# MLP first product in pairs of 64-row matmuls, with relays on ScalarE and the transposes moved to the second product

## The chip, the core and the metric

The kernel runs on one core of a Trainium2 chip. The core has a matrix engine (TensorE, PE in the profile; PEld is its weight load), VectorE (DVE), ScalarE (ACT), GpSimd (POOL) and a queue for transfers (SyncE, SP). TensorE writes into PSUM, eight banks of 128 partitions by 512 fp32 numbers; everything else lives in SBUF, 128 partitions wide. The metric is the device time of one execution in microseconds, lower is better. The time before is 827.49 us, the median of three runs (826.62 to 827.83).

## What is computed

Four layers over x of 2048 tokens by D = 576, in the order A, B, A, B. A is linear attention with 32 heads, B is an MLP with F = 4608 hidden units. Both take a layer norm first, and the norm inside B is applied to a row that has been normed already.

```python
def _B_ref(x, w1, b1, w2, b2):
    y = _layernorm(x, axis=-1)
    h = _gelu(jnp.einsum("bsd,df->bsf", y, w1) + b1)
    return jnp.einsum("bsf,fd->bsd", h, w2) + b2

x = x + _A_ref(_layernorm(x, axis=-1), A_wqkv, A_wo)
x = x + _B_ref(_layernorm(x, axis=-1), B_w1, B_b1, B_w2, B_b2)
x = x + _A_ref(_layernorm(x, axis=-1), A_wqkv, A_wo)
x = x + _B_ref(_layernorm(x, axis=-1), B_w1, B_b1, B_w2, B_b2)
```

`_A_ref` makes q, k, v from one product with `wqkv`, takes `phi` (an exponential linear unit plus one) of q and k, forms k-transposed-times-v and the sum of k per head, multiplies q with both, divides, and multiplies with `wo`.

## The kernel before

All products are in bf16 with fp32 sums in PSUM. Tokens are cut into 16 tiles of 128 rows, and for the MLP into four chunks of 512 tokens (`NCB`, `CB`), each of four tiles (`TPC`). D = 576 is held as five blocks of 128 rows (`KD`), of which the last has only 64 real rows. The normed activations stand transposed in one array, `yT`.

**The MLP (`LayerB`).** For each chunk, `m1_group` (line 458) is called for nine groups `g` of four blocks of 128 hidden units (`GF` = 4, `NF` = 36). A block needs four matmuls over 128 rows (line 469, 512 tokens wide) and one over the last 64 rows (line 474, "the tail"). The tail's activations stand in both halves of the partitions, and the tail weights of even blocks stand in rows 0 to 63 and of odd blocks in rows 64 to 127 of `w1_tail`, so that two tails can run side by side in two halves of the array. So a group is sixteen matmuls of 128 rows and then four of 64 rows. Two of the four sums of a group lie in single banks of the pool `ps_h` (three buffers), the other two in a pair of banks, tag `accA` for even and `accB` for odd groups. Four activations on ScalarE (line 478, gelu) take them to `hT`. `hT` shares its one buffer (tag `big`) with the work array `abig` of the attention layer.

Then comes the second product (line 499): for each of the four token tiles `j` of the chunk 36 x 2 matmuls of 288 columns, into the pair `accA` or `accB` by `j % 2`. VectorE adds the residual (line 278), and SyncE stores the row tile.

**The layer norm pipe (`LNPipe`).** A token tile goes through stages, one a `tick()`: load (-1), statistics on VectorE (0), power on GpSimd (1), a product on VectorE (2), the norm on VectorE and a copy of 64 columns on GpSimd (3), and in stage 4 five TensorE transposes into the one buffer `tp` (line 234) and a VectorE copy into `yT` (line 238). Ticks are called after each group of the first product and three times per token tile in the second. The next chunk's tiles are fed at g = 2, 4, 6, 8; their loads use the tag `xn`, which the residual uses as well.

**Order.** The framework's scheduler sorts the instructions of each engine by program order and by its own estimate of when they can start, and sets the semaphores; each engine then runs its list in order. Only the start-up transfers have an order by hand (`chained`). The first two groups of chunk 0 (g = 0 and 1) are issued from within the last steps of the attention layer (`make_a2_hook`), so their matmuls are mixed with the attention's output product (line 426).

Of the kernel before, what the change touches and what calls it, by code (L numbers as in the profile page):

```python
# [7 lines left out]
ACT = mybir.ActivationFunctionType  # L8
ALU = mybir.AluOpType
BF16 = mybir.dt.bfloat16  # L10
F32 = mybir.dt.float32
PSUM = bass.MemoryType.PSUM
DRAM = bass.MemoryType.DRAM

S, D, F, H, DH = 2048, 576, 4608, 32, 18
P = 128
NT = S // P
KD = 5
DPAD = KD * P
NF = F // P  # L20
# [6 lines left out]
NCB = S // CB  # L27
TPC = CB // P
CA = 512
NCA = S // CA  # L30
HALF = D // 2
# [4 lines left out]
def build(tc, A_x, A_wqkv, A_wo, B_w1, B_b1, B_w2, B_b2, out, dbg=None, n_layers=4):  # L36
    nc = tc.nc
    dbg = dbg or {}
    with ExitStack() as ctx:
# [54 lines left out]
        x0_tiles = {}  # L94

        NOSYNC = mybir.DependencyInfo(mybir.DependencyClass.NoSync, mybir.DependencyReason.SCHED_ONLY)
        chain = dict(last=None)

        def chained(inst):
            if chain["last"] is not None:  # L100
                tc.add_manual_dep(inst.ins, chain["last"], NOSYNC, reason="start-up DMA issue order")
            chain["last"] = inst.ins.name
            return inst

        def load_x0(t):
# [69 lines left out]
        class LNPipe:  # L175
# [7 lines left out]
            def busy(self):  # L183
                return len(self.items)

            def tick(self):
                for it in list(self.items):
                    st = it["stage"]
                    if st == -1:
                        xn = work.tile([P, D], F32, name="xn", tag="xn", bufs=3)  # L190
                        nc.sync.dma_start(out=xn[:], in_=x_d[it["load"]])
                        it["xt"] = xn
                    elif st == 0:
                        xt = it["xt"]
                        stt = work.tile([P, 2, 6], F32, name="ln_st", bufs=4)
                        nc.vector.bn_stats(out=stt[:, 0, :], in_=xt[:, 0:HALF])
                        nc.vector.bn_stats(out=stt[:, 1, :], in_=xt[:, HALF:D])
                        mv = work.tile([P, 2], F32, name="ln_mv", bufs=6)
                        nc.vector.bn_aggr(out=mv[:], in_=stt[:])
                        u = work.tile([P, 1], F32, name="ln_u", bufs=4)  # L200
                        if it["kind"] == "A":
                            nc.vector.tensor_scalar(out=u[:], in0=mv[:, 1:2], scalar1=EPS, scalar2=None, op0=ALU.add)  # L202
                        else:
                            nc.vector.tensor_scalar(out=u[:], in0=mv[:, 1:2], scalar1=1.0 + EPS, scalar2=EPS * EPS,
                                                    op0=ALU.mult, op1=ALU.add)
                        it["mv"], it["u"] = mv, u
                    elif st == 1:
                        rstd = work.tile([P, 1], F32, name="ln_rstd", bufs=6)
                        nc.gpsimd.tensor_tensor(out=rstd[:], in0=it["u"][:], in1=neg_half[:], op=ALU.pow)  # L209
                        it["rstd"] = rstd  # L210
                    elif st == 2:
                        nmr = work.tile([P, 1], F32, name="ln_nmr", bufs=4)
                        nc.vector.tensor_scalar(out=nmr[:], in0=it["mv"][:, 0:1], scalar1=-1.0,
                                                scalar2=it["rstd"][:, 0:1], op0=ALU.mult, op1=ALU.mult)
                        it["nmr"] = nmr
                    elif st == 3:
                        y = y_ring[state["ycnt"] % NY]
                        state["ycnt"] += 1
                        xt = it["xt"]
                        if it["norm"] == "act":  # L220
                            nc.scalar.activation(out=y[:, 0:D], in_=xt[:, 0:D], func=ACT.Identity,
                                                 scale=it["rstd"][:, 0:1], bias=it["nmr"][:, 0:1])
                        else:
                            eng = nc.vector if it["norm"] == "dve" else nc.gpsimd
                            eng.tensor_scalar(out=y[:, 0:D], in0=xt[:, 0:D], scalar1=it["rstd"][:, 0:1],
                                              scalar2=it["nmr"][:, 0:1], op0=ALU.mult, op1=ALU.add)
                        nc.gpsimd.tensor_copy(out=y[:, D:DPAD], in_=y[:, 4 * P:D])  # L227
                        it["y"] = y
                    elif st == 4:
                        y = it["y"]  # L230
                        t = it["t"]
                        tp = ps_tp.tile([P, KD, P], BF16, name="tp", tag="tp")
                        for k in range(KD):
                            nc.tensor.transpose(out=tp[:, k, :], in_=y[:, k * P:(k + 1) * P], identity=ident[:])  # L234
                        if it["evac"] == "act":
                            nc.scalar.copy(out=yT[:, :, t * P:(t + 1) * P], in_=tp[:])
                        else:
                            nc.vector.tensor_copy(out=yT[:, :, t * P:(t + 1) * P], in_=tp[:])  # L238
                        self.items.remove(it)
                        continue  # L240
                    it["stage"] = st + 1
# [44 lines left out]
        def layer_A(li, next_kind, pre_a1=None, a2_hook=None):  # L286
# [146 lines left out]
            for s in range(-2, NT + 1):  # L433
# [11 lines left out]
                if a2_hook is not None:  # L445
                    a2_hook(s)

        GF = 4
        NGRP = NF // GF

        class LayerB:
# [5 lines left out]

            def m1_group(self, c, g):
                if c not in self.hT:
                    self.hT[c] = big.tile([P, NF, CB], BF16, name="hT", tag="big")  # L460
                hT = self.hT[c]
                ctok = slice(c * CB, (c + 1) * CB)
                pair = ps_acc.tile([P, 2, 512], F32, name="hp_ps", tag=("accA", "accB")[g % 2])
                hps = [ps_h.tile([P, 512], F32, name="h_ps", tag="h") for _ in range(2)]
                dst = [hps[0][:], hps[1][:], pair[:, 0, :], pair[:, 1, :]]
                for n in range(GF):
                    f = g * GF + n
                    for k in range(KD - 1):
                        nc.tensor.matmul(dst[n], lhsT=w1_sb[:, k, f * P:(f + 1) * P], rhs=yT[:, k, ctok],  # L469
                                         start=(k == 0), stop=False)  # L470
                for n in range(GF):
                    half = slice(64 * (n % 2), 64 * (n % 2) + 64)
                    fc = (g * GF + n) // 2 * P
                    nc.tensor.matmul(dst[n], lhsT=w1_tail[half, fc:fc + P], rhs=yT[half, KD - 1, ctok],  # L474
                                     start=False, stop=True)
                for n in range(GF):
                    f = g * GF + n
                    nc.scalar.activation(out=hT[:, f, :], in_=dst[n], func=ACT.Gelu_apprx_tanh,  # L478
                                         bias=b1T[:, f:f + 1], scale=1.0)
                self.done[c] = g + 1  # L480

            def run(self):
                li, next_kind = self.li, self.next_kind
                for c in range(NCB):
                    for g in range(self.done.get(c, 0), NGRP):
                        self.m1_group(c, g)
                        if g in (3, 5):
                            prefetch_xo(li, c * TPC + (g - 3) // 2, add_b2=True)
                        if c + 1 < NCB and g in (2, 4, 6, 8):
                            t = (c + 1) * TPC + (g - 2) // 2  # L490
                            lnp.feed(None, t, "B", "dve", "dve", load_from=t)
                        lnp.tick()
                    hT = self.hT.pop(c)
                    for j in range(TPC):
                        t = c * TPC + j
                        acc = ps_acc.tile([P, 2, 512], F32, name="m2_ps", tag=("accA", "accB")[j % 2])
                        for f in range(NF):
                            for half in range(2):
                                nc.tensor.matmul(acc[:, half, 0:HALF], lhsT=hT[:, f, j * P:(j + 1) * P],  # L499
                                                 rhs=w2_sb[:, f, half * HALF:(half + 1) * HALF],  # L500
                                                 start=(f == 0), stop=(f == NF - 1))
                            if f % 12 == 6:
                                lnp.tick()
                            if f == 18 and j < 2:
                                prefetch_xo(li, c * TPC + 2 + j, add_b2=True)
# [47 lines left out]
        for li, kind in enumerate(kinds):  # L553
            nk = kinds[li + 1] if li + 1 < n_layers else None
            if kind == "A":
# [9 lines left out]
                while late_pads:  # L565
                    late_pads.pop(0)()
            else:
                lbs[li].run()
        lnp.drain()


# [45 lines left out]
```

## Time and profile before

| | |
|---|---|
| median of three runs | 827.49 us |
| span of the profiled execution | 822.3 us |
| median less span (what lies around the span) | 5.2 us |
| TensorE busy | 799.8 us (97%) |
| ScalarE busy | 326.1 us (40%) |
| VectorE busy | 276.2 us (34%) |
| GpSimd busy | 106.8 us (13%) |
| mean granted TensorE clock | 0.995 |

The page gives no device time of the profiled execution of its own other than its span, so the median is set beside it. A matmul of the profile lasts longer than the distance to the next one, because matmuls overlap in the array: 379 ns is the length of a 512-column matmul, and the starts of two in a row are 216 ns apart. A busy share of 97% therefore hides whatever gap is shorter than that overlap; the starts have to be read.

### The profile page before, as it was taken

Reading aid. Unit: us, or ns where it says so; the run is one execution under the profiler, and the core shown is the slowest. Engines: PE = TensorE matmul, PEld = TensorE weight load, DVE = VectorE, ACT = ScalarE, POOL = GpSimd, SP = SyncE. Lnnn points to the kernel's source line nnn. Section 1 sums busy time; section 2 is a strip of 40 time slices with the busy share of each in tenths; the row PEclk is TensorE's granted clock in tenths of the full one; section 3 lists DMA queues with packets and bytes.
Section 4 is the critical chain, followed back from the end, with each engine's and each line's share of the span. In section 5 each row is a group of like instructions: output and inputs, shape, how many; then the busy total and the mean of one; then the engine's idle time right before and its main releaser. Section 6 shows DMA issues by size and latency. Waiting matters only on the chain.

```text
span 822.3 us, 14103 instructions
## 1 busy us (share of the span) xinstructions
PE 799.8 (97%) x5844; PEld 510.9 (62%) x5878; DVE 276.2 (34%) x850; ACT 326.1 (40%) x600; POOL 106.8 (13%) x198
## 2 busy tenths in 40 slices
PE   5999999999999999999999999999999999999998
PEld 3787774486458547744877877536844863585376
DVE  5756974024204502310244598543201200010000
ACT  5687745501530351046027767452045015303510
POOL 6420301012102301210100000121200010011000
PEclk9999999999999999999999999999999999999999
DMA  9990543013002300100110035722200110011000
GB/s 229 280 299 1 174 132 107 0 59 102 15 1 68 106 1 29 59 29 1 59 58 1 2 95 181 225 64 60 64 22 15 42 47 0 1 55 34 0 23 22
DMA packets 42896, 56.81 MB, mean 69 GB/s; under 512 B 10256, under 2 KB 26896, under 8 KB 42832
## 3 DMA queue, kind: packets, MB, share of 16 engines
q1 hardware_dynamic: 42832, 55.91, 22.8%
q8 instruction: 46, 0.75, 0.4%
q14 instruction: 18, 0.15, 0.1%
HBM read 39.38 MB, written 16.52 MB: 68 GB/s over the span
## 4 chain that ended last, share of the span: by engine, by line
PE 88%; DVE 3%; ACT 3%; issue 1%; DMA 1%; POOL 1%; ACTq 0%; DVEq 0%; POOLq 0%
PE m_ps L499 33%; PE h_ps L469 15%; PE hp_ps L469 15%; PE q_ps L335 5%; PE k_ps L303 4%; PE wo_ps L426 3%; PE h_ps L474 3%; PE v_ps L314 2%; PE v_ps L311 2%; PE hp_ps L474 2%; ACT hT L478 2%; PE tp L234 2%; PE to_ps L416 1%; PE kvacc L327 1%; PE nd_ps L389 1%
## 5 line engine op out<-in xcount | busy, mean ns | idle before, releaser
L499 PE MATMUL m_ps<-w_sb,hT 128*128 128x288 bf16 x2304 | 287.9, 286 | 2.5 <-ACT hT L478 2.5
L499 PEld LDWEIGHTS <-hT 128*128 128x128 bf16 x2304 | 224.1, 98 | 59.9 <-issue 4.5
L478 ACT ACTIVATE hT<-h_ps,b1T 128x512 bf16<-128x512 f32 x144 | 91.2, 684 | 340.2 <-PE h_ps L474 340.2
L469 PEld LDWEIGHTS <-w_sb 128*128 128x128 bf16 x1152 | 107.9, 98 | 139.1 <-issue 21.7
L469 PE MATMUL hp_ps<-yT,w_sb 128*128 128x512 bf16 x563 | 135.5, 379 | 0.7
L469 PE MATMUL h_ps<-yT,w_sb 128*128 128x512 bf16 x555 | 134.8, 380 | 1.1
L478 ACT ACTIVATE hT<-hp_ps,b1T 128x512 bf16<-128x512 f32 x144 | 91.3, 694 | 0.0
L209 POOL TENSOR_TENSOR ln_rstd<-ln_u,neg_half 128x1 f32<-128x1 f32 x64 | 36.6, 572 | 371.3 <-DVE ln_u L202 219.8
L238 DVE COPY yT<-tp 128x640 bf16<-128x640 bf16 x40 | 19.6, 490 | 186.5 <-PE tp L234 186.5
L268 POOL TENSOR_TENSOR xo<-xo,b_bc 128x576 f32<-128x576 f32 x32 | 41.1, 1283 | 206.5 <-DMA xo<-x_d 206.4
L278 DVE TENSOR_TENSOR xbf<-m_ps,xo 128x576 bf16<-128x576 f32 x16 | 12.1, 754 | 141.7 <-PE m_ps L499 141.7
L335 PE MATMUL q_ps<-yT,wqkv_sb 128*126 128x512 bf16 (+1 forms) x200 | 51.7, 381 | 0.0
L426 PE MATMUL wo_ps<-wo_sb,abig 128*128 128x288 bf16 x320 | 46.7, 286 | 0.0
L303 PE MATMUL k_ps<-wqkv_sb,yT 128*128 128x288 bf16 x320 | 46.3, 293 | 0.0
L278 DVE TENSOR_TENSOR xn<-m_ps,xo 128x576 f32<-128x576 f32 x16 | 12.1, 758 | 99.2 <-PE m_ps L499 99.2
L251 ACT ACTIVATE phi_e<-k_ps 128x288 bf16<-128x288 f32 x64 | 26.8, 419 | 38.9 <-PE k_ps L303 35.6
L256 DVE TENSOR_TENSOR abig<-phi_a,phi_e 128x288 bf16<-128x288 bf16 (+2 forms) x104 | 36.0, 346 | 8.1 <-ACT phi_a L253 2.2
L254 DVE TENSOR_SCALAR phi_e<-phi_e 128x288 bf16<-128x288 bf16 (+2 forms) x104 | 29.7, 286 | 21.7 <-ACT phi_e L251 21.3
L426 PEld LDWEIGHTS <-abig 128*128 128x128 bf16 x320 | 29.6, 98 | 10.7 <-issue 1.3
L303 PEld LDWEIGHTS <-yT 128*128 128x128 bf16 x320 | 30.7, 100 | 8.0
L234 PE MATMUL tp<-ident,y_ring 128*128 128x128 bf16 x320 | 29.2, 222 | 4.5 <-POOL y_ring L227 1.9
L234 PEld LDWEIGHTS <-y_ring 128*128 128x128 bf16 x320 | 21.6, 99 | 18.1 <-issue 11.5
(73 smaller groups left out, 651.9 us busy)
## 6 DMA issues: line engine op xcount, KB each, us to landing
x_d<-xn SPq DMA_DIRECT2D x48, 288.0 KB, 2.2
xo<-x_d SPq DMA_DIRECT2D x48, 288.0 KB, 2.9
xn<-x_d SPq DMA_DIRECT2D x24, 288.0 KB, 3.0
w_sb<-in_B_w_dram SPq DMA_DIRECT2D x6, 864.0 KB, 11.0
xbf<-in_A_x_dram SPq DMA_DIRECT2D x32, 144.0 KB, 4.1
w_sb<-in_B_w_dram SPq DMA_DIRECT2D x9, 512.0 KB, 5.2
out_dram<-xbf SPq DMA_DIRECT2D x16, 144.0 KB, 1.8
wqkv_sb<-in_A_wqkv_dram SPq DMA_DIRECT2D x1, 1152.0 KB, 6.7
```

Source lines behind the costliest of these rows:

```text
L209: nc.gpsimd.tensor_tensor(out=rstd[:], in0=it["u"][:], in1=neg_half[:], op=ALU.pow)
L234: nc.tensor.transpose(out=tp[:, k, :], in_=y[:, k * P:(k + 1) * P], identity=ident[:])
L254: nc.vector.tensor_scalar(out=e[0:rows, 0:n], in0=e[0:rows, 0:n], scalar1=1.0, scalar2=1e-6, op0=ALU.min, op1=ALU.add)
L256: nc.vector.tensor_tensor(out=out_ap, in0=a[0:rows, 0:n], in1=e[0:rows, 0:n], op=ALU.max)
L268: nc.gpsimd.tensor_tensor(out=xo[:], in0=xo[:], in1=b2_bc[:], op=ALU.add)
L303: nc.tensor.matmul(kp[:, 0:HALF], lhsT=yT[:, k, tok], rhs=wqkv_sb[:, k, D + half * HALF: D + (half + 1) * HALF], start=(k == 0), stop=(k = ...
L335: nc.tensor.matmul(qp[0:GR[g], :], lhsT=wqkv_sb[:, k, GO[g]:GO[g] + GR[g]], rhs=yT[:, k, c * CA:(c + 1) * CA], start=(k == 0), stop=(k == ...
L426: nc.tensor.matmul(wp[:, half, 0:HALF], lhsT=oT[:, k, :], rhs=wo_sb[:, k, half * HALF:(half + 1) * HALF], start=(k == 0), stop=(k == KD - 1))
L469: nc.tensor.matmul(dst[n], lhsT=w1_sb[:, k, f * P:(f + 1) * P], rhs=yT[:, k, ctok], start=(k == 0), stop=False)
L474: nc.tensor.matmul(dst[n], lhsT=w1_tail[half, fc:fc + P], rhs=yT[half, KD - 1, ctok], start=False, stop=True)
L478: nc.scalar.activation(out=hT[:, f, :], in_=dst[n], func=ACT.Gelu_apprx_tanh, bias=b1T[:, f:f + 1], scale=1.0)
L499: nc.tensor.matmul(acc[:, half, 0:HALF], lhsT=hT[:, f, j * P:(j + 1) * P], rhs=w2_sb[:, f, half * HALF:(half + 1) * HALF], start=(f == 0), ...
```

## The change

The first product is issued entirely as matmuls of 64 rows. Each 128-row block becomes an upper half (rows 0 to 63) and a lower half (rows 64 to 127), and the tail goes to the half in which its weights stand: nine half matmuls per block, 36 per group, eighteen for each half of the array. They are issued alternately, upper and lower. The upper half takes the blocks in the order 0, 1, 2, 3 and the lower in the order 2, 3, 0, 1, so that at any moment they write different banks. Midway in the group the halves exchange banks. The hand-over is guarded by two one-column copies on ScalarE per group ("relays"): a relay waits for the matmul that ends the first use, and the first matmuls of the second use wait for the relay.

TensorE's instructions of the MLP are put into program order by hand (`pe`). The pairs `accA` and `accB` now alternate throughout (`next_acc`), so the second product's first tile does not take the pair that the last group used. Transposes are not issued in the ticks of the first product any more, and at most one token tile is transposed in a tick of the second. The next chunk's tiles are fed at g = 4 and 6 and in the second product at j = 0, f = 6 and 18, and their loads have a tag of their own (`xl`, two buffers).

```diff
+        relay_sb = const.tile([P, 2], F32, name="relay_sb")
+        nc.gpsimd.memset(relay_sb[:], 0.0)
...
+        def pe(inst):
+            if pe_chain["on"]:
+                if pe_chain["last"] is not None:
+                    tc.add_manual_dep(inst.ins, pe_chain["last"], NOSYNC, reason="TensorE order in the MLP")
+                pe_chain["last"] = inst.ins.name
             return inst
...
-            def tick(self):
+            def tick(self, transposes=1):
                 for it in list(self.items):
                     st = it["stage"]
+                    if st == 4:
+                        if transposes == 0:
+                            continue
+                        transposes -= 1
                     if st == -1:
-                        xn = work.tile([P, D], F32, name="xn", tag="xn", bufs=3)
+                        xn = work.tile([P, D], F32, name="xl", tag="xl", bufs=2)
...
+        def next_acc():
+            acc_turn["n"] += 1
+            return ("accA", "accB")[acc_turn["n"] % 2]
...
-                for n in range(GF):
+                def half_blocks(n, hi):
                     f = g * GF + n
-                    for k in range(KD - 1):
-                        nc.tensor.matmul(dst[n], lhsT=w1_sb[:, k, f * P:(f + 1) * P], rhs=yT[:, k, ctok],
-                                         start=(k == 0), stop=False)
...
+                    rows = slice(64 * hi, 64 * hi + 64)
+                    ops = [(n, w1_sb[rows, k, f * P:(f + 1) * P], yT[rows, k, ctok]) for k in range(KD - 1)]
+                    if f % 2 == hi:
+                        fc = f // 2 * P
+                        ops.append((n, w1_tail[rows, fc:fc + P], yT[rows, KD - 1, ctok]))
+                    return ops
+
+                upper = [op for n in (0, 1, 2, 3) for op in half_blocks(n, 0)]
+                lower = [op for n in (2, 3, 0, 1) for op in half_blocks(n, 1)]
...
+                relay_at = {last[(0, 0)]: (0, 2), last[(1, 3)]: (1, 3)}
+                starts = {first[(1, 0)]: 0, first[(0, 2)]: 2, first[(1, 1)]: 1, first[(0, 3)]: 3}
+                for i, (hi, n, wt, mv) in enumerate(order):
+                    mm = pe(nc.tensor.matmul(dst[n], lhsT=wt, rhs=mv, start=(seen[n] == 0), stop=(seen[n] == 8)))
+                    seen[n] += 1
+                    if i in starts:
+                        tc.add_manual_dep(mm.ins, relay_of[starts[i]], SYNC, reason="row tiles take turns on a PSUM bank")
+                    if i in relay_at:
+                        relay = nc.scalar.copy(out=relay_sb[:, 1:2], in_=relay_sb[:, 0:1])
+                        tc.add_manual_dep(relay.ins, mm.ins.name, SYNC, reason="row tiles take turns on a PSUM bank")
+                        for m in relay_at[i]:
+                            relay_of[m] = relay.ins.name
+                    if seen[n] == 9:
+                        f = g * GF + n
+                        nc.scalar.activation(out=hT[:, f, :], in_=dst[n], func=ACT.Gelu_apprx_tanh,
+                                             bias=b1T[:, f:f + 1], scale=1.0)
...
-                        if c + 1 < NCB and g in (2, 4, 6, 8):
-                            t = (c + 1) * TPC + (g - 2) // 2
-                            lnp.feed(None, t, "B", "dve", "dve", load_from=t)
-                        lnp.tick()
+                        if g in (4, 6):
+                            feed_next(c, (g - 4) // 2)
+                        lnp.tick(transposes=0)
...
-                        acc = ps_acc.tile([P, 2, 512], F32, name="m2_ps", tag=("accA", "accB")[j % 2])
+                        acc = ps_acc.tile([P, 2, 512], F32, name="m2_ps", tag=next_acc())
...
                             if f % 12 == 6:
+                                if j == 0 and f in (6, 18):
+                                    feed_next(c, 2 + f // 18)
                                 lnp.tick()
```

## The prediction

> **What bounds the kernel now.** I read the page's busy shares first, then the chain that ended last, then single stretches of the order of time, because only starts show what TensorE loses.
>
> ```profile
> PE 799.8 (97%) x5844; PEld 510.9 (62%) x5878; DVE 276.2 (34%) x850; ACT 326.1 (40%) x600; POOL 106.8 (13%) x198
> ...
> PE 88%; DVE 3%; ACT 3%; issue 1%; DMA 1%; POOL 1%; ACTq 0%; DVEq 0%; POOLq 0%
> ...
> L499 PE MATMUL m_ps<-w_sb,hT 128*128 128x288 bf16 x2304 | 287.9, 286 | 2.5 <-ACT hT L478 2.5
> L474 PEld LDWEIGHTS <-w_tail x288: 92/93/96, 118.4 to 782.2; 64*128 64x128 bf16 x144
> ```
>
> TensorE is the bound everywhere that the change touches; the other engines are below half. A gain must come out of TensorE's own list. One group of the first product in order of time, chunk 1 of the first MLP:
>
> ```profile
> 203.00 3.13 PEld L469 LDWEIGHTS <-w_sb 128*128 128x128 bf16 x16 [0.42 <-issue]
> 203.01 1.90 PE L469 MATMUL h_ps<-yT,w_sb 128*128 128x512 bf16 x8
> ...
> 204.74 1.89 PE L469 MATMUL hp_ps<-yT,w_sb 128*128 128x512 bf16 x8
> ...
> 206.56 0.11 PEld L474 LDWEIGHTS <-w_tail 64*128 64x128 bf16 x4 [0.42 <-issue]
> 206.57 0.39 PE L474 MATMUL h_ps<-yT,w_tail 64*128 64x512 bf16 x2
> 206.79 0.38 PE L474 MATMUL hp_ps<-yT,w_tail 64*128 64x512 bf16 x2
> 206.99 1.27 ACT L478 ACTIVATE hT<-h_ps,b1T 128x512 bf16<-128x512 f32 x2 [1.61 <-PE h_ps L474]
> 207.10 0.28 PEld L234 LDWEIGHTS <-y_ring 128*128 128x128 bf16 x5 [0.42 <-issue]
> 207.10 0.45 PE L234 MATMUL tp<-ident,y_ring 128*128 128x128 bf16 x5
> ```
>
> The reader is to see three things. Eight matmuls in 1.89 us, of which the last lasts 0.38, are 7 steps of 0.216. Two tails lie side by side: both pairs last as long as one matmul, and the pairs are 0.22 apart. And each change between 128 and 64 rows leaves a gap that the busy row hides: the eighth matmul starts at 204.74 + 1.89 - 0.38 = 206.25 and the first tail at 206.57, 0.31 later where 0.216 would do; from the second pair (206.79) to the transposes (207.10) again 0.31. So a change of rows costs some 0.094 us. Last, the seam from first to second product:
>
> ```profile
> 161.84 0.78 PE L499 MATMUL m_ps<-w_sb,hT 128*128 128x288 bf16 x5
> 162.33 0.10 PEld L234 LDWEIGHTS <-y_ring 128*128 128x128 bf16 x1
> 162.58 0.44 PE L234 MATMUL tp<-ident,y_ring 128*128 128x128 bf16 x5
> 162.59 1.27 ACT L478 ACTIVATE hT<-hp_ps,b1T 128x512 bf16<-128x512 f32 x2
> 162.86 0.65 PE L499 MATMUL m_ps<-w_sb,hT 128*128 128x288 bf16 x4
> 163.91 1.26 PE L499 MATMUL m_ps<-w_sb,hT 128*128 128x288 bf16 x9 [0.40 <-ACT hT L478]
> ```
>
> TensorE starts again 0.05 us after ScalarE's last gelu (162.59 + 1.27 = 163.86): group 8 and tile 0 share a pair of banks.
>
> **The change part by part.** The sum is made against the span of the one profiled execution, 822.3 us; the median of the runs, 827.49, is 5.2 above, and I carry that over as it is.
>
> *Matmul work.* Before, a group is 16 + 2 steps of 0.216 = 3.89 us; after, 18 pairs, also 3.89 if a pair takes one step. Nothing is saved here. Does a pair take one step? The two tail pairs start 227 ns apart, but the first step after any change of rows is longer in full-row rows too (226 for 216; transposes 66 for 56), so about 1 ns is left over. That is one step per group, and no row shows a long train of pairs. I take 2 ns a pair, 72 groups x 18 x 2 ns = +2.6 us; the ends are 0, and 10 ns (all of that longer step), +13.
>
> *Weight loads.* 36 a group for 20, one per 0.108 us. Transposes show loads 0.056 apart (five in 0.28), and all four tail loads are issued and done in 0.11 us, two of them for halves whose matmul had just begun. So they hide behind the matmuls: nothing. The Trainium skill, "TensorE: Matmul & The Clock Gate", Part 3, says otherwise: a weight load overlaps a matmul in flight only if it goes to another row group. By that rule each pair would expose a load of 93 ns, 1296 x 0.093 = +120 us, and the kernel would end near 940. The rows above contradict it, for full rows as well (each L469 load lies beside a matmul of the same rows), and I go by the rows.
>
> *Changes of rows removed.* The starts show 74 changes to 64 rows and 73 back, 147 x 0.094 = 13.8 us. After, each of eight chunks has one in and one out (16). The groups 0 and 1 in the attention's tail stay mixed with 128-row work; before, their matmuls come in about nine pieces between attention work, now every piece in 64 rows costs two changes: some 10 per layer, 20. Saved (147 - 36) x 0.094 = -10.4 us; ends -8 and -12.3.
>
> *The seam.* `next_acc` gives tile 0 the pair of group 7, whose gelus are long over. Gaps of the kind shown, over eight chunks: 3.5 us before line 499 and 1.9 us before the transposes of line 234 that wait there for `tp` or for their row. -5.4 us; ends -3.5 and -5.4. What is late next at the seam is the gelu of the last four blocks, needed by tile 0's f = 32, 64 matmuls x 0.1225 = 7.8 us later.
>
> *The relays.* 144 one-column copies on ScalarE. No row shows one; exponentials of 288 and 512 columns take 419 and 600 ns, a straight line through them gives 0.19 us at no columns. ScalarE has time (2.3 + 0.4 of 3.9 us a group), so the question is lateness, since both halves of the array stand behind a waiting matmul and ScalarE works in order. Clock a group from its first pair. ScalarE starts 0.41 us after the start of the matmul it waits for (206.57 to 206.99). Block 0 ends with the lower step 12: gelu at 2.59 + 0.41 = 3.01; the four gelus run 0.57 to 0.59 apart, so the last starts at 4.74, and relay 1 of the next group at 5.32, that is 1.43 on its clock (its own matmul, step 4, would let it go at 1.28). It ends by 1.62 to 1.74 (a gelu's end trails by 0.12), TensorE may go 0.05 later, at the latest at 1.79. It is wanted at step 9, 1.94. Relay 2 waits for step 8: 1.73 + 0.41 + 0.19 + 0.05 = 2.38, wanted at step 13, 2.81. So nothing, with 0.15 us and 0.43 us to spare; the first is the thinnest cover of the change. Beyond it every 0.1 us costs 64 groups (those behind another group) x 0.1 = 6.4 us. Upper end: 0.1 late, +6.4.
>
> *The groups within the attention's tail.* Relays stand in ScalarE's list with copies of 0.69 us (line 418), and gelus of group 0 can't start before `abig` is free (129.89 in the first layer). Group 1's second matmul now needs the pair `accB`, free only after the last residual (128.56 + 0.77 = 129.3); before, four matmuls of its block 0 could go ahead. And its relay 1 stands behind group 0's gelus, 129.89 + 4 x 0.575 + 0.24 = 132.4, where step 9 would come at 129.4 + 1.94 = 131.3. So up to 1 us and 1.1 us are lost per layer, +4 us for the two; lower end 0 (the earlier attention work moves up by as much), upper end +8.
>
> *Transposes, loads, order.* The same 40 groups of five transposes at 0.28 us; in the second product they change no rows. Ticks there are 24 x 0.1225 = 2.94 us apart. The tightest is the next chunk's fourth tile, whose norm stands behind another tile's transposes (0.28), a copy (0.49, after 0.25), its norm (0.57) and GpSimd's copy (0.24) with some 0.2 of hand-over: 2.0 of 2.94 us. The 24 loads (3.0 us to landing) move later on SyncE's queue; the fourth waits for the first-used `xl` buffers, and VectorE may stand up to 2 us for it in tile 0, ahead of tile 0's residual, whose pair is wanted only a tile (9 us) later. Nothing on the path; if the cover fails it is 0.67 us a seam, as before at 636.6, 4 us over six. The memset at the start is hidden by the wait for the first transfers.
>
> Sum: +2.6 - 10.4 - 5.4 + 0 + 4 + 0 = -9.2 us: span 813.1, time 818.3.
>
> **The rivals.**
> *Late relays (slower).* If ScalarE's chain from step 12 to step 9 of the next group is longer than I reckon, each group waits. It decides from 9.2 / 64 = 0.14 us of lateness, that is 0.3 us more than reckoned. Against it: every term but the copy is a row; for it: the margin is only 0.15. At 0.3 us late the time is 818.3 + 19 = 837; had a gelu of the same group come ahead of relay 2, it would be near 1 us a group, 880.
> *Pairs do not keep the step.* Break-even is (9.2 + 2.6) / 1296 = 9 ns a pair. At 20 ns: 818.3 + 23 = 842. For it: there are only two pairs in a row anywhere. Against: the second pair's 1 ns.
> *The hand-over brings the gap back.* If TensorE, held at a waiting matmul, can't load the lower half's weights in advance, a load (0.093) shows at one or both relays: +6 to +12, 824 to 830, about no change. Against: a satisfied wait costs nothing at line 469 now, and after the wait at 163.91 the next matmul follows at the usual distance.
> *It does not do what it says* (a copy between gelus makes ScalarE reload its tables, 1.28 us twice per relay): near 1100. The profile has four reloads, none at a copy.
>
> **How the numbers follow.** The forecast 0.62, with its own range 811 to 824 (sum of the low ends -12.3 - 5.4 = -17.7, and a few us up); the hand-over 0.11; late relays 0.11; pairs 0.12; the rest 0.04. About 0.2% (1.7 us) can be told from no change. Faster: 0.62, most of the hand-over, and small lateness, 0.73; same 0.05; slower 0.22. The range goes from 810 to 833, which leaves out the worse parts of relays and pairs.
>
> **What would show it.** Right: in a group no gap between rows, 18 pairs at 0.216 (3.89 us from group to group for 4.09 now), starts of upper and lower a few ns apart, no wait of the matmul for a relay, the second product following the last pair at about 0.31, transposes only among line 499. Wrong: TensorE waiting for ScalarE at step 9, pairs at 0.23 or more, or several us more than now between the attention's last product and group 2.

## The result: 908.4 us, slower by 9.8%, and one wait that was not in the sum

The changed kernel takes 908.41 us (median of 907.11 to 910.56) against 827.44 us, a ratio of 1.0984 with an interval of 1.0965 to 1.1003. The prediction was 818.3 us with a range to 833. The profiled execution has a span of 906.6 us for 822.3 before.

The page of the changed kernel, the lines that answer to those shown of before (busy time and share of each engine; the chain that ended last; groups of instructions with busy time, mean ns and the idle time ahead of them):

```profile
PE 801.6 (88%) x7030; PEld 538.2 (59%) x7030; DVE 270.4 (30%) x850; ACT 356.9 (39%) x746; POOL 106.2 (12%) x199
...
PE 79%; ACT 11%; DVE 4%; issue 2%; DMA 1%; POOL 1%; DVEq 0%; POOLq 0%; ACTq 0%
...
L513 PE MATMUL hp_ps<-yT,w_sb 64*128 64x512 bf16 x1152 | 274.1, 376 | 81.4 <-ACT hT L524 81.4
L551 PE MATMUL m_ps<-w_sb,hT 128*128 128x288 bf16 x2304 | 289.8, 286 | 0.0
```

TensorE is as busy as before (801.6 us for 799.8), so the work has not grown. What is new is idle time: 81.4 us ahead of the half matmuls into the pair of banks (`hp_ps`), ended by ScalarE's gelu (line 524). The chain of waits shows the same: ScalarE's share went from 3% to 11%. The seam, on the other hand, is clean: line 551, the second product, has no idle time ahead of it, where line 499 had 2.5 us.

The list of waits tells how often (us in total, times, longest):

```profile
PE hp_ps L513 <- ACT hT L524: 81.4, 72, 1.4
ACT relay_sb L518 <- PE hp_ps L513: 48.3, 72, 0.9
```

72 times is once a group. One group in order of time, the end of group 0 of chunk 1 in the first MLP (TensorE's and ScalarE's lines):

```profile
216.76 0.19 ACT L518 COPY relay_sb<-relay_sb 128x1 f32<-128x1 f32 x1 [0.68 <-PE hp_ps L513]
...
217.36 0.38 PE L513 MATMUL hp_ps<-yT,w_tail 64*128 64x512 bf16 x1
217.36 0.38 PE L513 MATMUL h_ps<-yT,w_sb 64*128 64x512 bf16 x1
217.56 0.69 ACT L524 ACTIVATE hT<-h_ps,b1T 128x512 bf16<-128x512 f32 x1 [0.62 <-PE h_ps L513]
218.15 0.68 ACT L524 ACTIVATE hT<-hp_ps,b1T 128x512 bf16<-128x512 f32 x1
218.88 0.37 PE L513 MATMUL hp_ps<-yT,w_sb 64*128 64x512 bf16 x1 [1.14 <-ACT hT L524]
218.89 0.39 PE L513 MATMUL h_ps<-yT,w_sb 64*128 64x512 bf16 x1
```

The pair at 217.36 is step 13 (the steps of a group are its 18 pairs, counted from 0): the upper half ends block 2 with its tail, the lower half begins block 1. Then TensorE stands until 218.88, the next step coming 1.52 us after this one where 0.216 would do: 1.30 us lost. It starts 0.05 us after the end of the gelu that reads block 2 (218.15 + 0.68 = 218.83). The relays have nothing to do with it: the second one was over at 216.95. So the matmul that waits is step 14, the first with which the upper half goes on with block 3, and it waits for the gelu of block 2. The two blocks lie in different banks, but in one PSUM tile, `pair`. 72 x 1.30 = 93.6 us, and 908.4 - 93.6 = 814.8.

The stages tell the same without the single wait. Read off the order of time, from the first matmul of one part to the first of the next, in us:

| kernel | first product, chunk 1 of MLP 1 | all of chunk 1, MLP 1 | all of chunk 1, MLP 2 | group 0 to the end of chunk 0, MLP 1 |
|---|---|---|---|---|
| before | 37.78 | 75.08 | 73.96 | 84.19 |
| after | 46.90 | 84.52 | 83.40 | 97.21 |

46.90 less nine times 1.30 is 35.2, and nine groups of 18 steps of 0.216 are 35.0.

### The profile page after: what moved, and what is told of

Its sections match the earlier page's. It is cut to its first block, busy times and chain, and to the rows that moved or that the text cites. A ratio compares the mean times of both kernels' runs of the same rounds, so it can differ in the third digit from the quotient of the medians.

```text
span 906.6 us, 16729 instructions
## 1 busy us (share of the span) xinstructions
PE 801.6 (88%) x7030; PEld 538.2 (59%) x7030; DVE 270.4 (30%) x850; ACT 356.9 (39%) x746; POOL 106.2 (12%) x199
## 4 chain that ended last, share of the span: by engine, by line
PE 79%; ACT 11%; DVE 4%; issue 2%; DMA 1%; POOL 1%; DVEq 0%; POOLq 0%; ACTq 0%
PE m_ps L551 31%; PE h_ps L513 15%; PE hp_ps L513 15%; ACT hT L524 10%; PE q_ps L351 4%; PE k_ps L319 3%; PE v_ps L330 2%; PE wo_ps L442 2%; PE v_ps L327 2%; PE tp L250 2%; DVE xn L294 1%; PE kvacc L343 1%; PE to_ps L432 1%; DVE o_ring L416 1%; PE nd_ps L405 1%
## 5 line engine op out<-in xcount | busy, mean ns | idle before, releaser
L513 PE MATMUL hp_ps<-yT,w_sb 64*128 64x512 bf16 x1152 | 274.1, 376 | 81.4 <-ACT hT L524 81.4
L513 PE MATMUL h_ps<-yT,w_sb 64*128 64x512 bf16 x1152 | 286.0, 377 | 0.0
L513 PEld LDWEIGHTS <-w_sb 64*128 64x128 bf16 x2304 | 137.5, 94 | 215.0 <-issue 104.5
L518 ACT COPY relay_sb<-relay_sb 128x1 f32<-128x1 f32 x144 | 27.4, 190 | 272.5 <-PE h_ps L513 224.0
L524 ACT ACTIVATE hT<-hp_ps,b1T 128x512 bf16<-128x512 f32 x144 | 98.4, 683 | 78.7 <-PE h_ps L513 78.7
L524 ACT ACTIVATE hT<-h_ps,b1T 128x512 bf16<-128x512 f32 x144 | 98.4, 683 | 45.0 <-PE h_ps L513 43.3
L513 PE MATMUL h_ps<-yT,w_tail 64*128 64x512 bf16 x144 | 54.1, 376 | 0.0
L513 PE MATMUL hp_ps<-yT,w_tail 64*128 64x512 bf16 x144 | 54.1, 376 | 0.0
L243 POOL COPY y_ring<-y_ring 128x64 bf16<-128x64 bf16 x64 | 15.4, 244 | 228.5 <-DVE y_ring L241 199.1
```

The costliest lines, as they stand in the source:

```text
L513: mm = pe(nc.tensor.matmul(dst[n], lhsT=wt, rhs=mv, start=(seen[n] == 0), stop=(seen[n] == 8)))
L518: relay = nc.scalar.copy(out=relay_sb[:, 1:2], in_=relay_sb[:, 0:1])
```

## The experiments

**The two theories.** A: the framework orders the accesses to a PSUM tile by the tile, not by the bank; a matmul that follows, in program order, a gelu on the other bank of its tile waits for that gelu. In the changed kernel the gelu of block 2 is issued as soon as block 2 has its nine halves (step 13), ahead of block 3's last four matmuls. B: the wait belongs to the hand-over of banks through the relays, wherever the blocks lie. The built program speaks for A; it names what each instruction waits for (abridged, in its order, steps 13 and 14; `hp_ps[0:]` and `hp_ps[512:]` are the two banks of one tile):

```
Matmult     hp_ps[0:]   upper, step 13, last of block 2
Matmult     h_ps        lower, step 13, first of block 1    its load waits for relay 2
Activation  hT<-hp_ps[0:]   gelu of block 2
Matmult     hp_ps[512:] upper, step 14, block 3             waits for: Activation hT<-hp_ps[0:]
```

**Blocks regrouped (e1_regroup).** The pair holds blocks 1 and 3, which both end in step 17.

```diff
-                dst = [hps[0][:], hps[1][:], pair[:, 0, :], pair[:, 1, :]]
+                dst = [hps[0][:], pair[:, 0, :], hps[1][:], pair[:, 1, :]]
```

> The changed kernel, but the pair of banks holds blocks 1 and 3 of a group (which both end with step 17) and the two single banks hold blocks 0 and 2. Theory A (block 3's last four matmuls wait for the gelu of block 2 because both lie in one PSUM tile and the framework orders accesses tile by tile): the 72 waits of 1.30 us go, 908.4 - 93.4 = 815 us, 812 to 820; groups 3.89 us apart. Theory B (what is late is the relay of the second hand-over, wherever the blocks lie): the wait before block 3 stays, 908 us. If relay 1 is late by what I reckoned as its thin margin, some us more than 815 and a wait at step 9.

Measured: 908.38 us (907.85 to 908.9), no gain at all in the time. By that number alone it is theory B. The trace says something else: the wait is no longer at step 14. It stands now before the very last half matmul of a group, the tail of block 1.

```profile
PE hp_ps L513 <- ACT hT L524: 77.9, 72, 3.3
...
222.66 0.69 ACT L524 ACTIVATE hT<-hp_ps,b1T 128x512 bf16<-128x512 f32 x1
223.40 0.37 PE L513 MATMUL hp_ps<-yT,w_tail 64*128 64x512 bf16 x1 [0.86 <-ACT hT L524]
```

In step 17 the upper half's matmul ends block 3, its gelu is issued at once, and only then comes the lower half's matmul, which ends block 1, in the same tile. Program order between two matmuls of one step was enough. That the time came out the same to 0.03 us is chance: the wait is a little shorter (the first product of chunk 1 takes 46.10 us for 46.90), and the granted TensorE clock was a little lower (0.990 to 0.992 in these four executions, 0.994 to 0.996 in those of the changed kernel). Theory A had been right on the cause and I had not followed it to the last instruction; theory B can't say why the wait moved.

**The gelu one matmul later (e2_gelu_later).** The blocks as in the changed kernel; block 2's gelu is issued after the first late matmul of block 3.

```diff
                     if seen[n] == 9:
+                        ready.append(n)
+                    for m in [m for m in ready if m != 2 or i >= first[(0, 3)]]:
+                        ready.remove(m)
```

> The changed kernel with its blocks where they were, but the gelu of block 2 is issued after the first late matmul of block 3 (step 14), so that this matmul no longer comes after it in program order. Theory A: the first of block 3's last four matmuls no longer waits; but the other three still follow that gelu in program order, and the gelu reads the tile after a matmul of block 3, so the wait may move by one step rather than go: between 815 and 925 us, with TensorE waiting for ScalarE at step 15, not 14. Theory B: nothing changes, a wait at step 14 and 908 us.

Measured: 894.43 us (893.96 to 894.68), 14.0 less than the changed kernel; 72 x 0.216 = 15.6. Step 14 runs, and the wait stands before step 15:

```profile
222.12 0.38 PE L514 MATMUL hp_ps<-yT,w_sb 64*128 64x512 bf16 x1
222.12 0.69 ACT L528 ACTIVATE hT<-h_ps,b1T 128x512 bf16<-128x512 f32 x1 [0.62 <-PE h_ps L514]
222.14 0.38 PE L514 MATMUL h_ps<-yT,w_sb 64*128 64x512 bf16 x1
222.71 0.68 ACT L528 ACTIVATE hT<-hp_ps,b1T 128x512 bf16<-128x512 f32 x1
223.44 0.37 PE L514 MATMUL hp_ps<-yT,w_sb 64*128 64x512 bf16 x1 [0.92 <-ACT hT L528]
```

The wait follows the place of the gelu in program order, as A says and B does not.

**Relays tripled in the regrouped kernel (e5_relay3).**

```diff
+                        for _ in range(2):
+                            relay = nc.scalar.copy(out=relay_sb[:, 1:2], in_=relay_sb[:, 0:1])
```

> e1_regroup with three copies in a row in place of each relay. A copy lasts 0.19 us on ScalarE and each waits for the one before. By my reckoning relay 1 then releases TensorE at 1.79 + 0.38 = 2.17 us of a group's clock, wanted at 1.94: 0.23 us late in 64 groups, +15 us over e1_regroup (830 us), and no wait at the second hand-over (2.76 for 2.81). If relay 1 has more to spare than 0.15 us, less: with 0.4 us to spare nothing.

Measured: 904.42 us (903.03 to 905.26), not dearer than e1_regroup. It was meant for a kernel without the wait; with the wait in place the first product of chunk 1 is 46.20 us for 46.10, so but for 0.10 us in nine groups the further copies are hidden by it. That shows only that relays were not what bounds a group here. The 4 us less go with the granted clock: e5's four executions had 0.994 to 0.996 for the 0.990 to 0.992 of e1, and 0.004 of 908 us is 3.6 us (an estimate). In the profiled execution of e1 the clock was 0.50 from 139.3 to 142.7 us, within the first product of chunk 0; in that of e5 it was 1.00 throughout that product.

**All gelus but one at the end (e6_gelu_end), and blocks regrouped with the last two gelus at the end (e7_regroup_end).** e6 leaves the blocks where they were and issues gelus 2, 3 and 1 after the group's last matmul. e7 regroups and issues gelus 3 and 1 there:

```diff
+                dst = [hps[0][:], pair[:, 0, :], hps[1][:], pair[:, 1, :]]
...
-                    if seen[n] == 9:
+                    if seen[n] == 9 and n not in (3, 1):
                         f = g * GF + n
                         nc.scalar.activation(...)
+                for n in (3, 1):
+                    f = g * GF + n
+                    nc.scalar.activation(...)
```

> The changed kernel with its blocks where they were; the gelus of blocks 2, 3 and 1 are issued after the group's last matmul. Theory A (a matmul that follows, in program order, a gelu of the other bank of its tile waits for it) as the last runs sharpened it: no matmul follows such a gelu any more, so the wait of 1.30 us goes (-93.4 us, 815); but now the gelu of block 2 comes after block 3's last matmul and waits for that, so the four gelus end later: the last starts at 5.24 us of the group's clock, relay 1 of the next group at 5.81 (1.92), TensorE is let go at 2.16 and wanted it at 1.94: 0.22 us late in 64 groups, +14 us: 829 us, 822 to 832. Rival (the wait comes from the relays): 908 us.

> The pair of banks holds blocks 1 and 3 (as in e1_regroup), and the gelus of blocks 3 and 1 are both issued after the group's last matmul; gelus 0 and 2 stay where they were. Theory A: no matmul waits for a gelu of its own group, the gelus run 0, 2, 3, 1 without a gap, and relay 1 is in time with 0.15 us to spare: 908.4 - 93.4 = 815 us, 811 to 820, groups 3.89 us apart. If instead relay 1 is late here too, 820 to 835. Rival (relays): 908 us.

Measured: e6 831.06 us (ratio to before 1.0044, 1.0029 to 1.0058), e7 821.05 us (0.9912, 0.9882 to 0.9942). With the wait gone 77 and 87 us come back; theory A stands. The first product of chunk 1 takes 37.01 us in e6 and 35.07 in e7. The 1.94 us between them, over the eight groups that follow another, are 0.24 us each, where 0.22 was reckoned for a relay behind a late gelu. In e6 TensorE's load now waits for the relay:

```profile
224.51 0.47 ACT L518 COPY relay_sb<-relay_sb 128x1 f32<-128x1 f32 x2
224.76 0.55 PEld L513 LDWEIGHTS <-w_sb 64*128 64x128 bf16 x8 [0.56 <-ACT relay_sb L518]
```

In e7 the group runs as the prediction had drawn it:

```profile
219.82 1.03 PE L513 MATMUL h_ps<-yT,w_sb 64*128 64x512 bf16 x8
220.10 1.27 ACT L528 ACTIVATE hT<-hp_ps,b1T 128x512 bf16<-128x512 f32 x2
...
221.24 0.21 ACT L518 COPY relay_sb<-relay_sb 128x1 f32<-128x1 f32 x1
221.55 0.38 PE L513 MATMUL hp_ps<-yT,w_tail 64*128 64x512 bf16 x1
221.76 1.03 PE L513 MATMUL h_ps<-yT,w_sb 64*128 64x512 bf16 x8
222.02 0.19 ACT L518 COPY relay_sb<-relay_sb 128x1 f32<-128x1 f32 x1 [0.57 <-PE hp_ps L513]
...
223.71 0.60 PE L513 MATMUL h_ps<-yT,w_sb 64*128 64x512 bf16 x4
```

From 219.82 to 223.71 is one group, 3.89 us. Eight half matmuls in 1.03 us are four pairs: three steps of 0.216 and the length of the last. Relay 1 starts at 1.42 us of the group's clock (1.43 reckoned) and ends at 1.63; step 9 comes at 1.94. With the 0.05 us from ScalarE to TensorE that leaves 0.26 us to spare.

**Relays tripled without the wait (e8_regroup_end_relay3).**

> e7_regroup_end with three copies in a row in place of each relay: +0.38 us to both. With 0.15 us to spare at relay 1 it is 0.23 us late in 64 groups: +15 us over e7_regroup_end, 830 us (825 to 835). Nothing if there was 0.4 us to spare.

Measured: 828.85 us (ratio to before 1.0017, 1.0 to 1.0035), 7.8 over e7 by the medians, and the first product of chunk 1 is 36.73 us for 35.07: 0.21 us for each of the eight groups, where 0.23 was expected. TensorE's load waits for the last of the three copies:

```profile
226.67 0.21 ACT L518 COPY relay_sb<-relay_sb 128x1 f32<-128x1 f32 x1
226.91 0.41 ACT L521 COPY relay_sb<-relay_sb 128x1 f32<-128x1 f32 x2
227.37 0.55 PEld L513 LDWEIGHTS <-w_sb 64*128 64x128 bf16 x8 [0.52 <-ACT relay_sb L521]
```

That 0.21 came so near 0.23 is in part luck. The three copies take 0.65 us (226.67 to 227.32) where one takes 0.21, so they add 0.44 and not 0.38; and the cover in e7 was 0.26 us, not 0.15. The total, 64 x 0.21 = 13 us, is more than the medians show, in part because e7's five executions fall in two sets by the granted clock: 817.38 and 817.84 us at 0.994, 821.05 to 823.33 at 0.990. The profiled executions of e7 and e8, both at 0.994, are 11.3 us apart (817.38 and 828.70). It confirms the thin cover: three relays of 0.19 us instead of one, and the whole gain over the kernel before is gone.

**What the parts are worth (e4_full_rows, e10_full_rows_hook, e9_regroup_end_hook, e11_hook_again).** e4 keeps all of the change but the half rows: the first product of the kernel before stands in `m1_group`, with TensorE's order by hand.

> The rest of the change alone: alternating pairs, transposes only in the second product, TensorE's order by hand, but the first product in full rows with the tails as before (no half matmuls, no relays). The wait at the seam goes (5.4 us before); the 147 changes of rows stay at 13.8 us: 827.4 - 5.4 = 822 us, 820 to 826. If the order by hand costs in the attention's tail, up to 828. The half rows themselves are then worth e1_regroup less this one: -7 us (815 against 822).

Measured: 827.88 us (ratio 0.9999, 0.9986 to 1.0013), not 822. The seam's gain is there, 74.39 us for chunk 1 of MLP 1 where it was 75.08, and 73.26 for 73.96 in MLP 2; but from group 0 to the end of chunk 0 it takes 86.64 us for 84.19 and 85.67 for 83.64. What is lost there, at the attention's tail, 2.5 and 2.0 us, eats what six or seven seams of 0.7 us bring.

e9 is e7 with the two groups within the attention's tail issued as before the change, e10 is e4 with the same: there the order by hand is left off, and in e9 the rows are full.

```diff
+                if not pe_chain["on"]:
+                    dst = [hps[0][:], hps[1][:], pair[:, 0, :], pair[:, 1, :]]
+                    ...  # full rows, tails and gelus as in the kernel before
+                    return
```

> e7_regroup_end, but groups 0 and 1 of chunk 0, the ones within the attention's tail, are issued as before the change: full rows and tails, no relays, no order by hand. If half rows, relays and order by hand cost 2.5 us there per layer (the difference from e4_full_rows to before in that stretch: 49.4 for 46.9 us), this is 5 us faster than e7_regroup_end: 810 us, 806 to 814. If the attention's tail is set by its own chain, the same.

> e4_full_rows (full rows and tails everywhere, alternating pairs, transposes only in the second product, order by hand in the MLP), but the two groups within the attention's tail without order by hand, as before the change. If the order by hand cost 2.5 us per layer there, this is 827.9 - 5 = 823 us, and the seam's 5.4 us come to light: 822 to 824, faster than before by 0.5%. If the order by hand costs nothing there, 828.

> e9_regroup_end_hook once more, beside e10_full_rows_hook on the same chip: 812 us. The two differ in the half rows of 68 groups alone (with relays and the pair's blocks regrouped), so the difference is what the half rows are worth where nothing waits: 64 to 68 groups x 0.19 us less 16 changes at the seams, 11 us.

Measured: e9 812.16 us, a ratio of 0.9817 (0.9787 to 0.9846): faster than both kernels. e11, the same kernel on another chip, 0.9838 (0.9816 to 0.986). e10 825.87 us, 0.9983 (0.997 to 0.9997), 2 us above the 822 to 824 that were expected. From group 0 to the end of chunk 0 the first MLP takes 84.22 us in e9 for 86.99 in e7, and 85.16 in e10 for 86.64 in e4, so the two groups are better left to the scheduler, by 2.8 us in half rows and 1.5 in full rows (2.2 and 1.1 in the second MLP). So the order by hand explains only a part of what e4 loses there: e10 does not come down to the 84.19 of before although its seam is shorter, and why the rest is lost I have not tried. Half rows where nothing waits: 0.9983 - 0.9838 of 827.3 us are 12.0 us, with 11 expected.

## Why the prediction was wrong

The step that failed is *the relays*, where the prediction asked what TensorE would wait for in a group and ended with "So nothing, with 0.15 us and 0.43 us to spare". That list of waits held the relays alone. It left out the waits that the framework puts between a gelu and a later matmul of the same PSUM tile. I had followed the banks, which is what the change's relays are built on; the waits follow the tile, and the program order of the instructions that touch it. The term is +93.6 us (72 x 1.30), and it turns 818.3 into 911.9; 908.4 was measured.

Nothing in the trace of before could show it, since there all of a group's matmuls are issued ahead of its gelus. The diff could: the gelu had moved into the loop over matmuls (`if seen[n] == 9`), and two of the four sums share a tile. The Trainium skill, "PSUM — Partial Sum Buffer", section "PSUM bank collisions raise a hardware error", asks for a guard by bank and quadrant and calls the guard by bank the simple version. The waits of this case are coarser than that, a tile of two banks; by the rule's own measure block 3 would have had no wait. No run here lets TensorE write one bank of a pair while ScalarE reads the other, so that it would go through on the chip stays open.

The rest of the sum, by its own steps, as e7 (the changed kernel without the wait, 821.05 us) and its kin show it. That e7 lies so near the predicted 818.3 is in part luck, since terms were off in both directions:

- *Matmul work.* +2.6 us taken; measured next to nothing. Nine groups in 35.07 us are 3.897 a group, 9 ns over 18 steps of 0.216. Both halves run side by side over long trains.
- *Weight loads.* Nothing, right. Two loads a step, each into rows whose matmul is in flight, cost no time: each group of e7 takes 3.89 us. The rule of the Trainium skill that was weighed there, with its +120 us, does not hold in these groups as it was put there. The same Part 3 of "TensorE: Matmul & The Clock Gate" also lets a load go ahead where it goes to a background weight buffer; no row here tells where a load went.
- *Changes of rows.* -10.4 us taken, -12.0 measured between e10 and e11, give or take some 2 us by their intervals. The price was right: chunk 1's first product has 17 changes fewer in e7 than in e4 and is 1.58 us shorter (35.07 for 36.65), 0.093 us each. The count was low: in before's trace the rows change 78 times each way, 156 and not 147.
- *The seam.* -5.4 us taken; e4's chunks 1 to 3 are shorter than before's by 3.9 us over six seams, some 5 us if the two of chunk 0 are alike (an estimate). Right in size.
- *The relays themselves.* The copy takes 0.19 us, as estimated from the two exponentials. Relay 1 has 0.26 us to spare rather than 0.15 (1.63 + 0.05 for 1.94). A relay that waits for its matmul alone starts 0.47 us after that matmul's start (221.55 to 222.02 in e7), where 0.41 was taken from a gelu; relay 2 has the room for it. That relay 1 is the thinnest cover was right: e6 and e8 fall off just there.
- *The groups within the attention's tail.* +4 us taken; e7 loses 2.8 and 2.2 us against e9, right in size. The relays were not the whole of it: e4, without relays or half rows, loses 1.5 and 1.1 us against e10 by the order by hand alone.
- *Transposes, loads and order.* Nothing, right for the middle chunks: the second product shows no wait for its transposes.

Of the rivals, *late relays* had the right engine and, with "had a gelu of the same group come ahead", much the right shape; but its 880 us was 28 short, its cause was a relay and not a PSUM tile, and it was given 0.11.

## What to carry to other kernels

When a change moves the reader of a PSUM tile in among the matmuls that fill it, list every pair of instructions that touch the same tile in program order, not the same bank: as this framework sets its waits, a later write waits for an earlier read, also of another bank. Put sums that are read at different times into different tiles, or issue the reads after the last write. Here two lines, which sums share a tile and where two gelus are issued, turned a loss of 81 us into a gain, and leaving the two groups in the attention's tail as they were made it 15 us.

## What the runs showed of the hardware that I had not expected

Two half matmuls side by side, with two loads a step, keep the step of a single full matmul over eighteen steps without loss (35.07 us for nine groups, 34.99 by steps of 0.216); I had allowed 2 ns a pair. And one of the five executions of e11 took 2920.86 us; the other four lie between 810.85 and 815.42, and the ratio is theirs. In its profile a 512-column matmul lasts 1.10 us instead of 0.38, while a gelu on ScalarE keeps its length (686 ns for 683 in e9). The list of cores gives a granted clock of 1.000 for it, but its page has no row for the clock, so the cause stays open.
